# Attention cross term on 64x64 quarters of the array, states without zeros, features in another order

## The chip, the core and the metric

The kernel runs on one NeuronCore of a Trainium2 chip. A core has TensorE (PE in the profile, matmuls; its weight loads are PEld), VectorE (DVE), ScalarE (ACT), GpSimd (POOL) and SyncE (SP, whose queue issues most DMAs); sixteen DMA engines move data between HBM and the on-chip memory SBUF. Matmuls write to PSUM, 128 partitions with eight banks of 512 fp32 numbers each. The metric is device time in microseconds (us) of one execution, lower is better.

## What is computed

```python
def _attn_ref(q, k, v):                       # 8 batches, 8 heads, 576 tokens, head size 64, fp32
    scores = scale * np.matmul(q, k.transpose(0, 1, 3, 2))
    gamma = 1.0 - 2.0 ** (-5.0 - np.arange(H, dtype=np.float32))
    rel = pos[:, None] - pos[None, :]
    Dmat = np.where(rel >= 0, gamma[:, None, None] ** rel[None, :, :], 0.0)
    ret = scores * Dmat[None, :, :, :]
    return np.matmul(ret, v).astype(np.float32)

def reference(**kwargs):
    attn_out = _attn_ref(**attn_kwargs)
    x = np.ascontiguousarray(attn_out.transpose(0, 2, 1, 3)).reshape(B * S, H * D)
    x = _moe_ref(x=x, **moe_kwargs)           # 4608 tokens of 512 features, 8 experts, one for each token
    return _moe2_ref(x=x, **moe2_kwargs)      # soft mixture, 8 experts with 4 slots each
```

The attention has no softmax: each score is only multiplied by a power of gamma, which depends on the head and the distance. So it can be done in chunks of tokens: what lies inside a chunk by a masked score matrix, and everything before the chunk by one 64x64 state for each head (a sum of outer products of keys and values), which the queries of the chunk multiply. That product is called the cross term here.

## The kernel before

The attention is the first stage. Two batches form a pair, and a pair has nine chunks of 128 tokens: four of the first batch (c = 0 to 3), four of the second (c = 4 to 7), and a ninth (c = 8) that holds the last 64 tokens of both. Four pairs make 36 chunks, counted by g. Heads go in four pairs p, with h = 0 or 1 for the head in the pair; a pair of heads fills the 128 partitions (2 x 64 features).

A loop over g writes out the work by hand, and each engine runs its instructions in that order. For PE an iteration is: scores of chunk g+1 (`emit_S`, L179, each head on one half of the array's rows), cross term of g (`emit_cross`, L198 for c = 8 and L200), logits of g-2 (L223, into `ps_m`), token-major transposes of g-1 (L216), masked scores times values of g (`emit_AV`, L205, added to the cross term in the PSUM tile `ps_x`), state update of g (`emit_state`, L191), router gate of g-1 (`emit_gate`, L212). There is no cross term for c = 0 and 4, where a batch begins, and no state update for c = 8.

DVE masks the scores (L182, `st_s`), multiplies `ps_x` by powers of gamma (L209, `xT`) and works off the routing of groups of 3 to 5 chunks in small steps (L230 to L257; `r_rs`, L252, reads the ranks that PE has put into `ps_m`). ACT copies `xT`'s transposes (`xr`), the states (L193) and the gate's output (`ls`). POOL scales the values (`vh`) and scatters the routing table. In chunks 25 to 32 ACT and DVE also split the first expert's weights in two parts (`wh`, L287, and `wl`, L288). Six `kqv` buffers of 1 MB hold keys, queries and values; SP issues the load of chunk g+5 at the head of iteration g and then the other transfers of that iteration, in program order.

In the state tiles a pair of heads has a 128x128 square with the two heads' 64x64 states on the diagonal and zeros elsewhere, so one matmul with 128 rows and 128 columns does the cross term of two heads. The zeros are written once by POOL, and two ACT copies write the diagonal blocks. `ps_x` is one PSUM bank, with two buffers. Behind the attention come products of expert weights (`ps_w`, `ps_wt`, L277 and L282, the latter using `ps_x`'s buffers late), then the loop over expert slots, then the soft mixture.

Of the kernel before, what the change touches and what calls it, by code (L numbers as in the profile page):

```python
# [4 lines left out]
F32=mybir.dt.float32; F32R=mybir.dt.float32r; BF16=mybir.dt.bfloat16; I32=mybir.dt.int32; U32=mybir.dt.uint32  # L5
AF=mybir.ActivationFunctionType; ALU=mybir.AluOpType; AX=mybir.AxisListType
ET=mybir.EngineType
PSUM=bass.MemoryType.PSUM; DRAM=bass.MemoryType.DRAM
B,H,S,D=8,8,576,64
NP=4  # L10
NCH=9
NT=B//2*NCH
E,DM,FF=8,512,1024
# [3 lines left out]
NPF=6  # L17
# [6 lines left out]
def host(inp):  # L24
    f=np.float32; c=np.ascontiguousarray
    o={}
# [9 lines left out]
    ids=chunks(np.broadcast_to(np.arange(NTOK).reshape(B,1,S),(B,H,S)))[:,0]  # L36
    mid=np.asarray(inp['moe_modality_id'])
    o['mid']=c(mid[ids].T)
    wg=np.zeros((128,4,32),f); wg[:,:,:E]=inp['moe_w_gate'].reshape(4,128,E).transpose(1,0,2)
    o['wg']=wg  # L40
    o['mb']=c(inp['moe_modality_bias'].reshape(1,2*E))
    o['w2']=c(inp['moe_w2'].reshape(E,8,128,512).transpose(0,2,1,3))
# [2 lines left out]

    o['m1']=c(inp['moe2_w1'].reshape(2,4,4,128,1024).transpose(0,2,3,1,4)).reshape(8,128,2,2048)

    o['w1']=c(np.concatenate([inp['moe_w1'].reshape(E,4,128,2,512).transpose(0,2,3,1,4).reshape(E,128,2,2048),o['m1'][NPF:NPF+1]]))
    o['m2']=c(inp['moe2_w2'].reshape(2,4,2,4,128,2,256).transpose(5,0,2,4,3,1,6).reshape(8,128,4096))

    g=1.0-2.0**(-5.0-np.arange(H))
    pw=g[:,None]**np.concatenate([np.arange(S),np.arange(512,S)])[None]
    o['gt']=c(np.concatenate([np.repeat(x,64,axis=1).transpose(1,0,2).reshape(128,-1) for x in (pw[:,:128].reshape(NP,2,128),pw[:,0:640:128].reshape(NP,2,5))],axis=1).astype(f))
    o['vtab']=c((1.0/(8.0*pw)).reshape(H,5,128).transpose(2,1,0).astype(f))
    p=np.arange(128)
    cm=np.zeros((128,1028),f)
# [23 lines left out]
def body(nc,tc,I,O):  # L80
    V=nc.vector; G_=nc.gpsimd; A=nc.scalar; PE=nc.tensor; SP=nc.sync
# [7 lines left out]
    with ctx, tc.manual_schedule():  # L89
        pool=lambda st,name,bufs,**k: st.enter_context(tc.tile_pool(name=name,bufs=bufs,**k))  # L90
# [7 lines left out]
        raw=[WP.tile([128,2048],F32,name=f"raw{j}") for j in range(2)]; w2=WP.tile([128,8,512],F32,name="w2")  # L98
        Wall=WP.tile([128,E,256],F32,name="Wall")
        AT=ExitStack(); A1=pool(AT,"A1",1); A2=pool(AT,"A2",2);  # L100
        PS=ExitStack(); PS2=pool(PS,"PS2",2,space=PSUM); PS1=pool(PS,"PS1",1,space=PSUM)
        def splita(h):
            for c in range(4):
                s=slice(c*512,c*512+512)
# [8 lines left out]
        pw=PS1.tile([128,512],F32,name="ps_wu",tag="ps_t")  # L113
# [16 lines left out]
        gt=A1.tile([128,5,NP,128],F32,name="gt"); gr=A1.tile([128,NP,5],F32,name="gr")  # L130
# [10 lines left out]
        def decay(c):  # L141
            for h in range(2 if c==4 else 1):
                s=slice(64*h,64*h+64) if c==4 else slice(0,128); w=s.stop-s.start
                G_.tensor_tensor(out=gt[:,c,:,s],in0=gt[:,0,:,0:w],in1=bc(gr[:,:,c],[128,NP,w],2),op=ALU.mult)
        state=[A1.tile([128,NP,128],F32,name=f"st{j}") for j in range(4)]
        for t in state: G_.memset(t,0.0)
        gk=A1.tile([128,NT,TW],F32,name="gk"); G_.memset(gk,0.0); idx=A1.tile([128,NT],U32,name="idx")
        cum=A1.tile([128,len(GR),E],BF16,name="cum"); spare=A1.tile([1,1],F32,name="spare")
        bias=A1.tile([128,NT,E],F32,name="bias")
# [11 lines left out]
        vh={}  # L161
        def pk(g,j): return kqv[g][:,j].rearrange("q (p t) -> q p t",p=NP)
        def pos_(g): return (0,1,2,3,0,1,2,3,4)[g%NCH]
        rq=[]
        def tick(n=1,stop=True):
            for _ in range(n):
                if rq and not (stop and rq[0].__name__=="rank"): rq.pop(0)()
# [5 lines left out]
        sts={}; xps={}; xTs={}; lss={}; pst={}  # L173
        def qT(g,p): return pk(g,1)[:,p]
# [9 lines left out]
        def emit_state(g):  # L184
            c=g%NCH; v=vh[g]; kt=kqv[g][:,3]
            if c%4==0: pst[0]=PS1.tile([128,NP,D],F32,name="ps_st")
            ps=pst[0]
            for p in range(NP):
                for h in range(2):
                    hh=2*p+h  # L190
                    PE.matmul(out=ps[64*h:64*h+64,p],lhsT=kt[:,hh*D:hh*D+D],rhs=v[:,hh],start=c%4==0 and p==0,stop=p==NP-1,skip_group_check=True)  # L191
            for h in range(2):
                r=slice(64*h,64*h+64); A.copy(out=state[2+c//4 if c%4==3 else c%2][r,:,r],in_=ps[r])  # L193
        def emit_cross(g):
            c=g%NCH; xps[g]=PS2.tile([128,NP,128],F32,name="ps_x")
            if c==8:
                for h in range(2):
                    for p in range(NP): PE.matmul(out=xps[g][:,p,64*h:64*h+64],lhsT=state[2+h][:,p],rhs=qT(g,p)[:,64*h:64*h+64],start=h==0 and p==0,stop=False,skip_group_check=True)  # L198
            elif c%4:
                for p in range(NP): PE.matmul(out=xps[g][:,p],lhsT=state[(c-1)%2][:,p],rhs=qT(g,p),start=p==0,stop=False)  # L200
        def emit_AV(g):
            c=g%NCH; ps=xps[g]; v=vh[g]
            for p in range(NP):
                for h in range(2):
                    PE.matmul(out=ps[64*h:64*h+64,p],lhsT=v[:,2*p+h],rhs=sts[g,h][:,p],start=c in(0,4) and p==0,stop=p==3,skip_group_check=c==8)  # L205
            for h in range(2): sts.pop((g,h))
        def emit_x(g):
            t=A2.tile([128,NP,128],F32,name="xT")
            V.tensor_tensor(out=t,in0=xps.pop(g),in1=gt[:,pos_(g)],op=ALU.mult); xTs[g]=t; tick()  # L209
        def emit_gate(g):  # L210
            lp=PS1.tile([128,128],F32,name="ps_gt")
            for j in range(4): PE.matmul(out=lp[32*j:32*j+32],lhsT=wg[:,j],rhs=xTs[g][:,j],start=True,stop=True)  # L212
# [65 lines left out]
            if c==3:  # L278
                t=A1.tile([128,256],F32,name="wt",bufs=2); A.copy(out=t,in_=wps.pop(e)); wts[e]=t
        def emit_WT(e,late=False):  # L280
            pt=PS2.tile([128,256],F32,name="ps_wt",tag="ps_x") if late else PS1.tile([128,256],F32,name="ps_wt",tag="ps_t"); t=wts.pop(e)
            for h in range(2): PE.transpose(out=pt[:,h*128:h*128+128],in_=t[:,h*128:h*128+128],identity=ident)  # L282
            A.copy(out=Wall[:,e],in_=pt)
        def split(h,cs=range(4)):
# [417 lines left out]
```

## Time and profile before

| | us |
|---|---|
| median of three runs | 666.62 (663.51 to 666.94) |
| the profiled execution, its own time | 665.61 |
| its span in the profile | 664.0 |
| PE busy | 613.2 |
| DVE, ACT, POOL busy | 319.0, 220.1, 247.7 |

The span is what the profiler saw, from the program's first instruction to its last. Times of rows are counted from its start. The attention is over at about 178 us; the first expert's transposes begin at 198.05 us. An fp32 matmul of the program is two PE instructions in the trace, each with its own weight load.

### The profile page before, as it was taken

The page shows a single profiled execution, that of the slowest core. Times are in us where ns is not written, and L with a number is a line of the kernel's source. Part 1 is how long each engine was busy: PE and PEld are TensorE (multiplying, and loading weights), DVE is VectorE, ACT ScalarE, POOL GpSimd, SP SyncE. Part 2 cuts the span into 40 slices and gives each one's busy share as a digit, 9 for nine tenths or more (in the row PEclk, how much of TensorE's full clock was granted, in tenths as well). Part 3 has the DMA queues.
Part 4 walks back from the last instruction along what each step waited for, and adds up shares of the span by engine and source line. Part 5 has one row for each costly group of instructions (what it writes and reads, how often), then busy time and mean ns, then how long its engine had stood idle before and what let it go on. Part 6 is the DMA issues. An engine that isn't in the chain of part 4 may idle for free. (4 is left out here: it accounts for less than half of the span.)

```text
span 664.0 us, 17074 instructions
## 1 busy us (share of the span) xinstructions
PE 613.2 (92%) x5866; PEld 461.1 (69%) x5866; DVE 319.0 (48%) x934; ACT 220.1 (33%) x577; POOL 247.7 (37%) x355
## 2 busy tenths in 40 slices
PE   7999999999969999988999999999998999669984
PEld 5888888888637766755677777777775777453453
DVE  2355555567434434566544544555555544322343
ACT  1333333344315233354233233332353233211332
POOL 4524445355536432466244334433455344110000
PEclk7999999999988999988999999999999999888995
DMA  8999999985928860144654444444404401857888
GB/s 291 414 378 386 418 387 323 352 317 208 394 90 332 287 245 16 37 146 161 258 162 144 142 149 153 162 163 151 163 21 161 162 11 51 294 211 282 356 284 286
DMA packets 48244, 148.53 MB, mean 224 GB/s; under 512 B 12276, under 2 KB 23935, under 8 KB 37888
## 3 DMA queue, kind: packets, MB, share of 16 engines
q1 hardware_dynamic: 41936, 132.60, 55.3%
q0 software_dynamic: 6192, 14.53, 6.3%
q8 instruction: 55, 0.90, 0.6%
q14 instruction: 61, 0.50, 0.2%
HBM read 291.93 MB, written 27.71 MB: 481 GB/s over the span
## 5 line engine op out<-in xcount | busy, mean ns | idle before, releaser
L472 PE MATMUL ps_L<-wh,xl 128*128 128x512 f32 x624 | 212.3, 412 | 0.9 <-ACTq L529 0.9
L472 PEld LDWEIGHTS ps_L<-wh,xl 128*128 128x128 f32 x624 | 116.0, 191 | 38.6 <-issue 16.9
L472 PE MATMUL ps_L<-wl,xl 128*128 128x512 f32 x312 | 126.5, 405 | 4.9 <-PEq L529 1.5
L472 PEld LDWEIGHTS ps_L<-wl,xl 128*128 128x128 f32 x312 | 59.4, 190 | 32.1 <-issue 22.0
L476 DVE TENSOR_SCALAR hh<-ps_L,gi 128x512 f32<-128x512 f32 x39 | 29.3, 750 | 97.4 <-PE ps_L L472 97.3
L182 DVE TENSOR_TENSOR st_s<-ps_s,cm 128x512 f32<-128x512 f32 x72 | 47.7, 683 | 38.2 <-PE ps_s L179 31.9
L170 POOL TENSOR_TENSOR vh<-kqv,vtab 128x512 f32<-128x512 f32 x36 | 37.3, 1036 | 71.1 <-PE ps_st L191 51.2
L494 ACT ACTIVATE z<-ps_z,mt 32x128 f32<-32x128 f32 x39 | 14.0, 358 | 148.2 <-DVE mt L493 148.2
L508 POOL TENSOR_SCALAR cy<-cx,cm 128x32 f32<-128x32 f32 x39 | 14.4, 369 | 123.9 <-DVE cm L507 119.6
L509 POOL DMA_INDIRECT cs<-cy,ui x39 | 42.2, 1083 | 16.5 <-POOL cy L508 13.3
L179 PE MATMUL ps_s<-kqv 64*128 64x128 f32 x576 | 44.1, 292 | 2.0 <-DVE st_s L182 1.6
L260 POOL DMA_INDIRECT tb<-gk,idx x36 | 36.0, 1001 | 19.2 <-issue 4.9
L179 PEld LDWEIGHTS ps_s<-kqv 64*128 64x128 f32 x576 | 36.8, 193 | 8.5 <-issue 3.6
L481 PE MATMUL ps_h<-cs__103,hh 128*128 128x128 f32 x312 | 41.3, 276 | 0.0
L209 DVE TENSOR_TENSOR xT<-ps_x,gt 128x512 f32<-128x512 f32 x36 | 24.8, 690 | 32.4 <-PE ps_x L205 29.2
L205 PE MATMUL ps_x<-st_s,vh 128*64 128x128 f32 x576 | 40.3, 283 | 0.0
L217 ACT COPY xr<-ps_t 128x512 f32<-128x512 f32 x36 | 21.0, 585 | 57.9 <-PE ps_t L216 57.9
L475 ACT ACTIVATE hh<-ps_L,gi 128x512 f32<-128x512 f32 x39 | 26.9, 689 | 32.1 <-PE ps_L L472 32.1
L453 POOL DMA_INDIRECT xr__2862<-xd,ui x28 | 29.4, 1051 | 20.2 <-POOL ui L452 8.7
L481 PEld LDWEIGHTS ps_h<-cs__103,hh 128*128 128x128 f32 x312 | 36.2, 143 | 0.1
L205 PEld LDWEIGHTS ps_x<-st_s,vh 128*64 128x64 f32 x576 | 31.4, 139 | 6.1 <-issue 6.1
L193 ACT COPY st<-ps_st 64x256 f32<-64x256 f32 x64 | 23.4, 366 | 29.5 <-PE ps_st L191 28.9
(238 smaller groups left out, 1017.7 us busy)
## 6 DMA issues: line engine op xcount, KB each, us to landing
raw<-in_w SPq DMA_DIRECT2D x79, 1024.0 KB
w<-in_w SPq DMA_DIRECT2D x38, 2048.0 KB
kqv<-in_qkv SPq DMA_DIRECT2D x28, 1024.0 KB
m<-in_m SPq DMA_DIRECT2D x19, 1024.0 KB
xd<-xr SPq DMA_DIRECT2D x32, 256.0 KB
wh<-mx SPq DMA_DIRECT2D x8, 1024.0 KB
wl<-mx SPq DMA_DIRECT2D x8, 1024.0 KB
w2T<-in_w2T SPq DMA_DIRECT2D x12, 512.0 KB
```

The costliest lines, as they stand in the source:

```text
L170: G_.tensor_tensor(out=t,in0=kqv[g][:,2].rearrange("p (h d) -> p h d",h=H),in1=bc(vtab[:,pos_(g)],[128,H,D],2),op=ALU.mult)
L179: r=slice(64*h,64*h+64); PE.matmul(out=pss[h][:,p],lhsT=pk(g,0)[r,p],rhs=pk(g,1)[r,p],start=True,stop=True)
L182: V.tensor_tensor(out=st,in0=pss[h],in1=bc(masks[g%NCH],[128,NP,128],1),op=ALU.mult)
L205: PE.matmul(out=ps[64*h:64*h+64,p],lhsT=v[:,2*p+h],rhs=sts[g,h][:,p],start=c in(0,4) and p==0,stop=p==3,skip_group_check=c==8)
L209: V.tensor_tensor(out=t,in0=xps.pop(g),in1=gt[:,pos_(g)],op=ALU.mult); xTs[g]=t; tick()
L260: nodep(G_.indirect_dma_start(out=tb,out_offset=bass.IndirectOffsetOnAxis(ap=idx[:,k:k+1],axis=0),in_=gk[:,k],in_offset=None),"tb")
L453: G_.indirect_dma_start(out=xg[i%3],out_offset=None,in_=xd,in_offset=bass.IndirectOffsetOnAxis(ap=u,axis=0),bounds_check=NTOK-1,oob_is_err ...
L472: PE.matmul(out=ps,lhsT=a[:,c],rhs=w[h][:,s],start=n==0,stop=n==11); n+=1; m+=1
L475: if h==0: A.activation(out=d,in_=q,func=AF.Relu,scale=g)
L476: else: V.tensor_scalar(out=d,in0=q,scalar1=0.0,scalar2=g,op0=ALU.max,op1=ALU.mult)
L481: for c in range(4): PE.transpose(out=ps[:,c],in_=hh[i%2][:,2*half+c//2,(c%2)*128:(c%2)*128+128],identity=ident)
L509: nodep(G_.indirect_dma_start(out=cs,out_offset=bass.IndirectOffsetOnAxis(ap=gi[i][1],axis=0),in_=y,in_offset=None,bounds_check=NTOK-1,oob ...
```

## The change

The cross term is done by a 64x64 matmul for each head, with the state on half of the array's rows (by h) and the result on half of its columns (by p%2): four heads lie on the four quarters. A state tile is [128,4,64] and needs no zeros, and one ACT copy writes it. `ps_x` is [128,2,512], two banks of which 256 columns each are used: the head h of a pair picks the bank, since the two row halves write at the same time. It comes from the pool with one buffer, where it had two. The features of a token get another order, (p%2 and head size) on partitions, (h, p//2) along the tile; the router's weights, the first expert layer and the gamma table are permuted to match on the host. The loops of `emit_AV` are nested the other way round.

```diff
+    perm=np.arange(DM).reshape(2,2,2,D).transpose(2,0,1,3).reshape(-1)
+    wg=np.zeros((128,4,32),f); wg[:,:,:E]=inp['moe_w_gate'][perm].reshape(4,128,E).transpose(1,0,2)
...
-        PS=ExitStack(); PS2=pool(PS,"PS2",2,space=PSUM); PS1=pool(PS,"PS1",1,space=PSUM)
+        PS=ExitStack(); PS1=pool(PS,"PS1",1,space=PSUM)
...
-        state=[A1.tile([128,NP,128],F32,name=f"st{j}") for j in range(4)]
-        for t in state: G_.memset(t,0.0)
+        state=[A1.tile([128,NP,D],F32,name=f"st{j}") for j in range(4)]
...
+            A.copy(out=state[2+c//4 if c%4==3 else c%2],in_=ps)
+        def xo(g,p,h): return xps[g][64*(p%2):64*(p%2)+64,h,128*(p//2):128*(p//2)+128]
+        def emit_cross(g):
+            c=g%NCH; xps[g]=PS1.tile([128,2,512],F32,name="ps_x")
+            for a in range(2) if c==8 else (0,) if c%4 else ():
+                t=slice(64*a,64*a+64) if c==8 else slice(0,128)
+                for p in range(NP):
+                    for h in range(2):
+                        r=slice(64*h,64*h+64)
+                        PE.matmul(out=xo(g,p,h)[:,t],lhsT=state[2+a if c==8 else (c-1)%2][r,p],rhs=qT(g,p)[r,t],start=a==0 and p<2,stop=False,skip_group_check=True)
+        def emit_AV(g):
+            c=g%NCH; v=vh[g]
             for h in range(2):
-                r=slice(64*h,64*h+64); A.copy(out=state[2+c//4 if c%4==3 else c%2][r,:,r],in_=ps[r])
-        def emit_cross(g):
-            c=g%NCH; xps[g]=PS2.tile([128,NP,128],F32,name="ps_x")
-            if c==8:
-                for h in range(2):
-                    for p in range(NP): PE.matmul(out=xps[g][:,p,64*h:64*h+64],lhsT=state[2+h][:,p],rhs=qT(g,p)[:,64*h:64*h+64],start=h==0 and p==0,stop=False,skip_group_check=True)
-            elif c%4:
-                for p in range(NP): PE.matmul(out=xps[g][:,p],lhsT=state[(c-1)%2][:,p],rhs=qT(g,p),start=p==0,stop=False)
-        def emit_AV(g):
-            c=g%NCH; ps=xps[g]; v=vh[g]
-            for p in range(NP):
-                for h in range(2):
-                    PE.matmul(out=ps[64*h:64*h+64,p],lhsT=v[:,2*p+h],rhs=sts[g,h][:,p],start=c in(0,4) and p==0,stop=p==3,skip_group_check=c==8)
+                for p in range(NP):
+                    PE.matmul(out=xo(g,p,h),lhsT=v[:,2*p+h],rhs=sts[g,h][:,p],start=c in(0,4) and p<2,stop=p>1,skip_group_check=True)
             for h in range(2): sts.pop((g,h))
         def emit_x(g):
             t=A2.tile([128,NP,128],F32,name="xT")
-            V.tensor_tensor(out=t,in0=xps.pop(g),in1=gt[:,pos_(g)],op=ALU.mult); xTs[g]=t; tick()
+            V.tensor_tensor(out=t.rearrange("q (h n) t -> q h (n t)",h=2),in0=xps.pop(g)[:,:,0:256],in1=gt[:,pos_(g)].rearrange("q (h n) t -> q h (n t)",h=2),op=ALU.mult); xTs[g]=t; tick()
...
-            pt=PS2.tile([128,256],F32,name="ps_wt",tag="ps_x") if late else PS1.tile([128,256],F32,name="ps_wt",tag="ps_t"); t=wts.pop(e)
+            pt=PS1.tile([128,256],F32,name="ps_wt",tag="ps_x") if late else PS1.tile([128,256],F32,name="ps_wt",tag="ps_t"); t=wts.pop(e)
```

No engine gets its blocks in another order. What stands inside the cross term's block changes, and what it waits for. On PE, in the iteration of a chunk near the start, before, with the semaphores that an instruction waits for (Activation is ACT's, Pool is POOL's):

```order
L200 MATMUL ps_x<-kqv,st_132 128x128 [waits Activation_49]
L200 MATMUL ps_x<-kqv,st_132 128x128 x3
L223 MATMUL ps_m<-cs__103,ls 128x8 [waits Activation_49]
L216 MATMUL ps_t<-cs__103,xT 128x128 [waits DVE_49]
L216 MATMUL ps_t<-cs__103,xT 128x128 x3
```

And the same place now (the line numbers are one higher from here on):

```order
L201 MATMUL ps_x<-kqv,st_129 64x128 [waits DVE_49,Activation_49]
L201 MATMUL ps_x<-kqv,st_129 64x128 x7
L224 MATMUL ps_m<-cs__100,ls 128x8 [waits Activation_49]
L217 MATMUL ps_t<-cs__100,xT 128x128 x4
L206 MATMUL ps_x<-st_s,vh 64x128 [waits Pool_49]
```

Four matmuls have become eight, and DVE's `xT` of the chunk before, which the transposes waited for, is now waited for by the first matmul of the cross term. On ACT, in two iterations, before:

```order
L193 COPY st_131<-ps_st 64x4x64 x2
L213 COPY ls<-ps_gt 128x128
L217 COPY xr<-ps_t 128x512
L193 COPY st_132<-ps_st 64x4x64 x2
L213 COPY ls<-ps_gt 128x128
```

And now:

```order
L192 COPY st_128<-ps_st 128x256
L214 COPY ls<-ps_gt 128x128
L218 COPY xr<-ps_t 128x512
L192 COPY st_129<-ps_st 128x256
L214 COPY ls<-ps_gt 128x128
```

The two state copies of each chunk are one, and what stands behind them keeps its place.

## Rows read from the trace of the kernel before

**Rows 1.** The page: busy time by engine (PE's line), granted clock in 40 slices.
```profile
PE 613.2 (92%) x5866; PEld 461.1 (69%) x5866; DVE 319.0 (48%) x934; ACT 220.1 (33%) x577; POOL 247.7 (37%) x355
...
PEclk7999999999988999988999999999999999888995
```

**Rows 2.** Busy time in stretches, us from the span's start; the columns are named.
```profile
core 0: us, PE busy (x) PEld busy (x) DVE busy (x) ACT busy (x) POOL busy (x), PEclk, DMA share, GB/s
0.00:50.00 50.00, 46.02 (x593) 38.61 (x595) 19.94 (x38) 13.33 (x32) 20.38 (x33) 0.93 0.96 361
50.00:60.00 10.00, 10.00 (x162) 8.47 (x162) 5.40 (x13) 3.23 (x8) 3.38 (x5) 1.00 1.03 382
...
13.00:178.00 165.00, 163.06 (x2443) 141.16 (x2439) 90.33 (x224) 60.62 (x152) 76.51 (x114) 1.00 0.95 358
190.00:200.00 10.00, 3.87 (x41) 2.06 (x40) 2.02 (x8) 2.11 (x6) 4.26 (x7) 0.78 0.26 64
```

**Rows 3.** Waits of PE, 10 to 200 us: total us, times, longest.
```profile
PE ps_m L223 <- DVE r_rs L252: 1.3, 3, 0.5
PE ps_x L200 <- ACT st L193: 0.7, 1, 0.7
```

**Rows 4.** Timeline, one chunk: start, us, engine, line, what; then idle time before.
```profile
122.80 0.63 PE L191 MATMUL ps_st<-vh,kqv 128*64 128x64 f32 x16
123.02 0.69 DVE L209 TENSOR_TENSOR xT<-ps_x,gt 128x512 f32<-128x512 f32 x1 [1.46 <-PE ps_x L205]
123.36 0.16 PEld L212 LDWEIGHTS ps_gt<-xT,wg 128*32 128x32 f32 x8
123.72 0.97 PEld L179 LDWEIGHTS ps_s<-kqv 64*128 64x128 f32 x16 [0.20 <-issue]
124.81 0.97 PEld L200 LDWEIGHTS ps_x<-kqv,st 128*128 128x128 f32 x8
125.70 0.30 PEld L223 LDWEIGHTS ps_m<-cs__103,ls 128*128 128x128 f32 x2
```

**Rows 5.** Timeline, the cross term of the first ninth chunk (c = 8).
```profile
47.31 1.86 PEld L198 LDWEIGHTS ps_x<-kqv,st 128*128 128x128 f32 x16
...
49.09 0.30 PEld L223 LDWEIGHTS ps_m<-cs__103,ls 128*128 128x128 f32 x2
```

**Rows 6.** Timeline, the iteration behind the first ranked routing group.
```profile
56.36 1.16 PE L200 MATMUL ps_x<-kqv,st 128*128 128x128 f32 x8
...
57.07 0.19 DVE L252 TENSOR_TENSOR r_rs<-ps_m,r_ob 128x40 f32<-128x40 f32 x1
...
57.40 0.36 PE L223 MATMUL ps_m<-cs__103,ls 128*128 128x8 f32 x2
```

**Rows 7.** Timeline, the same behind the fifth group, where weights are split too.
```profile
137.87 0.62 ACT L287 CAST wh<-raw 128x512 fp32r<-128x512 f32 x1
...
138.53 0.69 DVE L288 TENSOR_TENSOR wl<-raw,wh 128x512 fp32r<-128x512 f32 x1 [1.37 <-ACT wh L287]
...
140.07 0.36 PE L223 MATMUL ps_m<-cs__103,ls 128*128 128x8 f32 x2 [0.41 <-DVE r_rs L252]
```

**Rows 8.** Timeline, the first cross term.
```profile
15.11 0.76 ACT L193 COPY st<-ps_st 64x256 f32<-64x256 f32 x2
...
15.92 1.16 PE L200 MATMUL ps_x<-kqv,st 128*128 128x128 f32 x8 [0.66 <-ACT st L193]
```

**Rows 9.** Timeline, from the last weight transposes to the first expert's.
```profile
192.36 0.37 ACT L283 COPY Wall<-ps_wt 128x256 f32<-128x256 f32 x1
192.50 0.20 PEld L282 LDWEIGHTS ps_wt<-cs__103,wt 128*128 128x128 f32 x2 [0.42 <-ACT wt L279]
...
193.13 0.27 DVE L397 MEMSET Gs<- 128x257 f32 x1 [6.60 <-PE ps_wt L282]
...
198.05 0.48 PE L459 MATMUL ps_xT<-cs__103,xr__2862 128*128 128x128 f32 x1 [5.11 <-DMA xr__2862<-xd,ui]
```

**Rows 10.** Timeline of SP's queue, 41 to 53 us, and PE at 64.67 us.
```profile
41.37 0.33 SPq L123 DMA_DIRECT2D kqv<-in_qkv  x1
41.79 9.34 SPq L159 DMA_DIRECT2D tb<-w2T  x9
...
52.39 1.05 SPq L123 DMA_DIRECT2D kqv<-in_qkv  x1
...
64.67 1.16 PE L179 MATMUL ps_s<-kqv 64*128 64x128 f32 x16
```

More of the change, by code (lines that the diff above doesn't have):

```diff
@@ L38, in host @@
     o['mid']=c(mid[ids].T)
-    wg=np.zeros((128,4,32),f); wg[:,:,:E]=inp['moe_w_gate'].reshape(4,128,E).transpose(1,0,2)
+    perm=np.arange(DM).reshape(2,2,2,D).transpose(2,0,1,3).reshape(-1)
+    wg=np.zeros((128,4,32),f); wg[:,:,:E]=inp['moe_w_gate'][perm].reshape(4,128,E).transpose(1,0,2)
     o['wg']=wg
@@ L46, in host @@
     o['m1']=c(inp['moe2_w1'].reshape(2,4,4,128,1024).transpose(0,2,3,1,4)).reshape(8,128,2,2048)
-    o['w1']=c(np.concatenate([inp['moe_w1'].reshape(E,4,128,2,512).transpose(0,2,3,1,4).reshape(E,128,2,2048),o['m1'][NPF:NPF+1]]))
+    o['w1']=c(np.concatenate([inp['moe_w1'][:,perm].reshape(E,4,128,2,512).transpose(0,2,3,1,4).reshape(E,128,2,2048),o['m1'][NPF:NPF+1]]))
     o['m2']=c(inp['moe2_w2'].reshape(2,4,2,4,128,2,256).transpose(5,0,2,4,3,1,6).reshape(8,128,4096))
@@ L52, in host @@
     pw=g[:,None]**np.concatenate([np.arange(S),np.arange(512,S)])[None]
-    o['gt']=c(np.concatenate([np.repeat(x,64,axis=1).transpose(1,0,2).reshape(128,-1) for x in (pw[:,:128].reshape(NP,2,128),pw[:,0:640:128].reshape(NP,2,5))],axis=1).astype(f))
+    o['gt']=c(np.concatenate([np.repeat(x,64,axis=1).transpose(1,0,2).reshape(128,-1) for x in [y.reshape(2,2,2,-1).transpose(2,0,1,3).reshape(4,2,-1) for y in (pw[:,:128],pw[:,0:640:128])]],axis=1).astype(f))
     o['vtab']=c((1.0/(8.0*pw)).reshape(H,5,128).transpose(2,1,0).astype(f))
```

## Prediction

> **What bounds the kernel now.** I read the page first: TensorE (PE) is busy for 92% of the span, no other engine for half of it, and the granted clock is full for almost all of it [rows 1]. The change lies in the attention stage alone, so I read the time in stretches next: from 13 to 178 us PE is busy for 163.06 of 165 us at granted clock 1.00, the 2.4 GHz level, but the sixteen DMA engines have a share of 0.95 there too, and 1.03 in the stretch at 50 us [rows 2]. Both could be the limit. The list of waits decides for PE: from 10 to 200 us it waited 1.3 us for DVE's `r_rs` and 0.7 us for ACT's state copy, and no wait for a `kqv` load stands there [rows 3]. So in this stage the sum of PE's work is the time, and a nanosecond saved there counts unless another engine is next in line.
>
> The timeline of one chunk gives the prices [rows 4]. Counted from the first weight load of a block to that of the next: cross term 124.81 to 125.70 = 0.89 us, scores (L179) 123.72 to 124.81 = 1.09, the state block 122.80 to 123.36 = 0.56, the gate 123.36 to 123.72 = 0.36. An fp32 matmul stands in the trace as two instructions, so the cross term's 4 are 8 rows: 0.89/8 = 0.111 us for one pass of 128 columns through the array; I call it a step. The scores have 16 instructions on 64 rows each, in pairs on the two row halves: 8 steps = 0.89, and 0.20 more. The gate has 8 on 32 array columns each, four side by side: 2 steps = 0.22, and 0.14 more. So row halves do run in pairs, column quarters do run four at a time, and what is left, 0.14 to 0.20, is the price of going from one division of the array to another (drain, and the first weights loaded in the open). The cross term pays none now, since the logit matmul behind it uses the whole array too.
>
> **The change, part by part.**
>
> *Plain cross terms.* Chunks 1, 2, 3, 5, 6, 7 of four batch pairs, 24 in all. Now 8 matmuls on 64x64 quarters, 16 instructions. If four run at a time they are 4 steps = 0.44, plus one more change of division behind them, 0.17 as the middle of 0.14 and 0.20: 0.61. Saved 0.89 - 0.61 = **0.28** each (0.25 to 0.31). No row shows row and column halves at once; the pairs and fours above are the nearest.
>
> *Six of the 24 give little.* Where a routing group was ranked in the iteration before, the next logit matmul writes `ps_m`, from which DVE's `r_rs` still has to read. At 56 us: cross at 56.36, `r_rs` 57.07 to 57.26, logit at 57.40, just when the cross term would have let it go (56.36 + 1.00) [rows 6]. A shorter cross term there becomes a wait. I found six such places (55, 73, 96, 114, 137, 156 us). Four give about 0.03 each. In the last two DVE comes later still, PE already waits 0.41, and the way to `r_rs` leads over ACT's `wh` copy and DVE's `wl` [rows 7]; ACT now makes two state copies of 64x256 in 0.76 us and then one of 128x256. A copy of 128x256 out of PSUM takes 0.37 elsewhere [rows 9], as long as one half does, so `wh` comes 0.37 earlier and these two give 0.37 each. Six together: **0.8**. The other 18 give 18 x 0.28 = **5.0**.
>
> *Chunk 8 of each pair*, the two tails of 64 tokens: 8 matmuls on the whole array, 16 instructions, 47.31 to 49.09 = 1.78 us [rows 5]. That is 0.111 a step although only 64 columns pass: the 128-column weight load sets it. Then 16 matmuls on quarters, 8 steps with 64 weight columns and 64 moving ones. The state block has just these sizes in pairs: 0.56 for 8 steps with a change, 0.053 to 0.07 a step. At 0.06: 0.48 + 0.17 = 0.65, saved 1.13, times four = **4.5** (bounds: 1.2 each at 0.053; 0.7 each if a step stays at 0.111).
>
> *State.* The copy loses its second half. At the first cross term PE waits 0.66 for the second copy [rows 8]; one copy ends 0.38 earlier: **0.4**. Elsewhere the state has been there before the scores end, and the other 31 second copies of 0.37 cost nothing. The zeroing of four state tiles by POOL at the start is covered by the wait for the first load.
>
> *One buffer in place of two.* `ps_x` takes two banks (a row half writes its own bank), so there is one of it, and the cross term must wait until DVE's `xT` of the chunk before has read it. `xT` ends at 123.02 + 0.69 = 123.71, the cross term begins at 124.81 [rows 4]: 1.10 us of cover, made of state, gate and scores, none of which shrinks. Cost 0. Without that cover it would be one `xT`, 0.69, per chunk. Queued behind it on PE would be logit, token transposes and AV, for which ACT and then the stores wait. At the very end the last two weight transposes (L282) share this tile: the second starts at 192.50 now and would wait for ACT's `Wall` copy, 192.36 + 0.37 = 192.73, and everything up to the first gather (PE waits until 198.05) hangs behind it [rows 9]: **-0.3**.
>
> AV's eight matmuls come in another order, still alternating column halves: 0. DVE reads as many elements of `ps_x`: 0. The permuted weights are made on the host.
>
> *Loads.* The saving makes PE use `kqv` earlier while the DMA engines are full. The tightest place is chunk 13: its load is issued at 52.39, behind nine pieces of `tb` that held the queue from 41.79, and its scores begin at 64.67 [rows 10]. By 50 us 361 GB/s x 50 = 18.1 MB had moved, then 382 GB/s [rows 2]; I count 20.9 MB issued up to and with that load, which makes it land near 57.5, about 7 us ahead. PE will have gained some 3.5 us by then. Cost 0; 2 us if my count is 5 us off.
>
> Sum: 5.0 + 0.8 + 4.5 + 0.4 - 0.3 = 10.4. The profiled execution took 665.61 (span 664.0), so 655.2; it is 1.0 under the median of the three runs, 666.62, and I take **655.6**.
>
> **Rivals.**
>
> *A. Instructions set the pace, not columns.* The state block's 32 matmuls and weight loads in 0.56 could be an issue limit: 0.035 us per matmul row. Then a plain cross term takes 16 x 0.035 + 0.17 = 0.73 (saves 0.16), a tail one 32 x 0.035 + 0.17 = 1.29 (saves 0.49): 2.9 + 0.8 + 2.0 + 0.1 = 5.8, about 660. Against it: the gate passes 8 in 0.22, 0.027 each, and 128-column steps explain that alone. The Trainium skill, page "TensorE: Matmul & The Clock Gate", section on 56 ns against 53.3 ns, says that with hardware decoding off the sequencer spends about 62 ns on each matmul; by that figure, an estimate, 16 would need 0.99 us and 32 would need 1.98, and the kernel would take about 673. This trace does not agree, the state block has a matmul every 35 ns, so I give that case 0.01.
>
> *B. Only pairs run together.* Cross 8 x 0.111 + 0.17 = 1.06, 0.17 worse; tails 16 x 0.06 + 0.17 = 1.13, 0.65 better. -3.1 - 0.6 + 2.6 + 0.1 = -1.0: 666.6, no change. For it: no row of two row halves and two column halves at once, with four moving streams to four quarters. Against: the scores write two banks at once, the gate reads four streams at once.
>
> *C. The quarters run one by one (slower).* Cross 16 x 0.111 + 0.17 = 1.95, 1.06 worse, times 24; tails 32 x 0.06 + 0.17 = 2.09, 0.3 worse: 26 us, 692. With a step of s for 128 columns and 0.54 s for 64, the gain is 18 x (0.72 - 4 s) + 4 x (1.61 - 4.3 s) + 0.9 = 20.3 - 89 s: above s = 0.23, twice what I assume, the change loses.
>
> *D. The freed time meets loads.* If the rate of 358 to 382 GB/s [rows 2] cannot follow chunks that are 0.28 shorter, PE waits for `kqv` near chunks 13 to 17, and 2 to 4 us of the 10 are lost: 658 to 660.
>
> **How the numbers follow.** My forecast 0.70, with its own range 652 to 658 (bounds above, and the three runs lie 3.4 us apart); a gain above it 0.03; A and D together 0.12; B 0.09; C 0.05; the 62 ns case 0.01. Leaving out the low end, most of B and C gives a range of 651 to 661. What a measurement of this kernel can tell from no change is about 0.5%, 3.3 us: faster means below 663.3. Forecast, larger gain, A and D are faster: 0.85; B is the same: 0.09; C with the 62 ns case is slower: 0.06.
>
> **What the profile after would show.** Cross blocks of 0.6 us from first weight load to the next block's, 0.65 in chunk 8; logit matmuls waiting for `r_rs` at all six places, some 0.25 us more at the first four; a chunk of 4.36 us in place of 4.64; no idle time of PE before the cross block on `xT`, and none before scores on `kqv`; the first gather's transpose near 188 in place of 198. Cross blocks of 1.1 or more would be B or C. The prediction is wrong if the later stage does not move to the left by what attention saves, for instance because the clock falls elsewhere at the turn: that stretch has 0.78 granted already [rows 2].

## The result, and the profile after

The changed kernel took 652.74 us, median of four runs (650.26 to 654.82), against 665.07 us (661.62 to 666.94) for the kernel before in the four runs beside it: a ratio of 0.984 [0.980, 0.987], 12.3 us less. A later set of runs of the same changed kernel gave 648.84 against 662.02, 0.980 [0.975, 0.985]. The profiled execution took 651.03 us, span 649.4, against 665.61 and 664.0 before.

From the page: TensorE has 14.9 us less to do and still the same share of the span, 92% [rows 1].

```profile
PE 598.3 (92%) x6122; PEld 441.1 (68%) x6122; DVE 319.1 (49%) x934; ACT 208.5 (32%) x545; POOL 245.9 (38%) x351
...
PEclk8999999999979999988999999999999999889997
```

One chunk after, from the timeline, in the order of [rows 4], with the masked scores times values (L206) of this chunk and the next at its ends:

```profile
113.19 0.85 PEld L206 LDWEIGHTS ps_x<-st_s,vh 128*64 128x64 f32 x16 [0.17 <-issue]
...
114.34 0.69 DVE L210 TENSOR_TENSOR xT<-ps_x,gt 128x512 f32<-128x512 f32 x1 [0.73 <-PE ps_x L206]
...
115.04 0.97 PEld L179 LDWEIGHTS ps_s<-kqv 64*128 64x128 f32 x16 [0.20 <-issue]
...
116.13 0.43 PEld L201 LDWEIGHTS ps_x<-kqv,st 64*64 64x64 f32 x16
...
116.73 0.30 PEld L224 LDWEIGHTS ps_m<-cs__100,ls 128*128 128x128 f32 x2 [0.17 <-issue]
...
117.53 0.53 PEld L206 LDWEIGHTS ps_x<-st_s,vh 128*64 128x64 f32 x10 [0.17 <-issue]
```

The cross block lasts 116.13 to 116.73 = 0.60 us, where it was 0.89; the scores are still 1.09. The chunk lasts 117.53 - 113.19 = 4.34. DVE's `xT` ends at 115.03 and the next cross term starts at 116.13, so the cover of the single `ps_x` is 1.10 us, as before. The cross term of the first ninth chunk, from the timeline of PE's weight loads, is 0.63 where [rows 5] have 1.78:

```profile
47.37 0.56 PEld L201 LDWEIGHTS ps_x<-kqv,st 64*64 64x64 f32 x32
48.00 0.30 PEld L224 LDWEIGHTS ps_m<-cs__100,ls 128*128 128x128 f32 x2
```

PE's waits from 10 to 200 us, the first four lines and the one on the weight transposes, to hold against [rows 3]:

```profile
PE ps_m L224 <- DVE r_rs L253: 3.1, 7, 0.6
PE ps_x L206 <- POOL cum L155: 2.2, 1, 2.2
PE ps_xT L460 <- DMA xr__2950<-xd,ui: 1.8, 1, 1.8
PE ps_L L473 <- ACTq L530: 0.9, 1, 0.9
...
PE ps_wt L283 <- ACT Wall L284: 0.5, 1, 0.5
```

The wait for the state copy is gone, that for `r_rs` has grown from 1.3 to 3.1, no `kqv` load and no `xT` has come in. The line of 2.2 us on POOL is new, and the wait for the first gather (`xr`) is 1.8 us where it was 5.11 [rows 9].

To see where the 14.6 us between the two profiled spans went, I cut both at PE instructions that both have: the masked scores times values of chunks 1, 5 and 35, and the first expert's transposes. Starts are read from the timeline; the table holds their differences, in us, for all kernels that ran, the experiments included.

| kernel | start to chunk 1 | 1 to 5 | 5 to 35 | 35 to expert | expert to end |
|---|---|---|---|---|---|
| before | 17.44 | 17.66 | 138.85 | 24.10 | 465.91 |
| after | 15.22 | 20.54 | 129.44 | 21.09 | 463.06 |
| after, once more | 17.12 | 16.77 | 129.44 | 21.51 | 460.80 |
| order by pairs (e3) | 17.10 | 18.02 | 129.82 | 20.46 | 465.34 |
| order by quarters (e10) | 15.80 | 20.26 | 129.96 | 21.34 | 465.40 |
| two halves (e7) | 17.26 | 18.48 | 143.35 | 19.39 | 462.96 |
| padded states (e2) | 18.21 | 16.77 | 129.43 | 24.54 | 464.45 |
| before, with a pad (e9) | 17.37 | 17.66 | 138.83 | 20.14 | 463.95 |
| preparation moved (e1) | 17.17 | 16.77 | 129.44 | 20.95 | 465.01 |
| ranking earlier (e4) | 16.50 | 20.26 | 128.74 | 20.99 | 464.88 |
| both of these (e6) | 16.41 | 16.77 | 127.78 | 20.30 | 466.38 |
| two state copies (e8) | 16.89 | 17.91 | 130.25 | 20.29 | 466.50 |

The changed kernel gained 9.41 us in chunks 5 to 35, as the cross-term part of the prediction has it. But it also gained 3.01 in the stretch to the first expert, where the prediction has a loss of 0.3, and lost 2.88 in chunks 1 to 5, where it has a gain. The first and last columns vary by 3 and 6 us between kernels that hardly differ there, the two runs of the changed kernel among them, so single values in them are not read as effects.

The loss first. The timeline of POOL and PE around chunk 4, and the stretches at the start and around chunk 4:

```profile
27.30 0.22 POOL L154 CAST mf<-mid 128x36 f32<-128x36 int32 x1 [7.18 <-DMA mid<-in_mid]
...
28.78 1.05 POOL L170 TENSOR_TENSOR vh<-kqv,vtab 128x512 f32<-128x512 f32 x1
...
29.88 1.93 PE L206 MATMUL ps_x<-st_s,vh 128*64 128x128 f32 x16 [2.17 <-POOL cum L155]
```

```profile
core 0: us, PE busy (x) PEld busy (x) DVE busy (x) ACT busy (x) POOL busy (x), PEclk, DMA share, GB/s
5.00:17.00 12.00, 10.49 (x141) 8.84 (x140) 5.13 (x8) 1.14 (x3) 4.90 (x5) 0.86 1.01 362
29.00:36.00 7.00, 6.12 (x82) 5.16 (x84) 1.98 (x3) 0.77 (x3) 5.18 (x8) 0.76 1.00 378
30.00:33.00 3.00, 3.00 (x40) 2.68 (x40) 0.69 (x1) 0.24 (x1) 2.63 (x5) 0.50 1.04 401
```

POOL stood still for 7.18 us until the load of `mid` landed; only behind that preparation did it scale chunk 4's values (`vh`, to 29.83), and PE waited 2.17 us for them. Right behind this wait the granted clock is low: 0.50, the 1.2 GHz level, from 30 to 33 us and 0.76 over 29 to 36 us, and the block of 16 that takes 1.09 at full clock takes 1.93. The kernel before has the same load, preparation and values in this order, but its chunk 4 began only at 30.46. In this run PE started early: 5 to 17 us had a granted clock of 0.86.

Then the gain at the turn to the experts, from the timeline, to hold against [rows 9]; the first line is the first gather before, which [rows 9] do not have, the others are after:

```profile
194.84 1.07 POOL L453 DMA_INDIRECT xr__2862<-xd,ui  x1 [5.05 <-DVE xr__2862 L427]
```

```profile
177.78 0.27 DVE L398 MEMSET Gs<- 128x257 f32 x1
...
183.04 1.07 POOL L454 DMA_INDIRECT xr__2950<-xd,ui  x1 [1.00 <-DMA gi<-tb]
...
184.03 0.44 PE L283 MATMUL ps_wt<-cs__100,wt 128*128 128x128 f32 x2 [0.46 <-ACT Wall L284]
...
186.29 0.66 PE L460 MATMUL ps_xT<-cs__100,xr__2950 128*128 128x128 f32 x4 [1.82 <-DMA xr__2950<-xd,ui]
```

The last weight transposes do wait for ACT's copy, 0.46 us, as foretold. But DVE's clearing of `Gs`, which in the kernel before stood 6.60 us for these transposes and had the rest of DVE's clearing behind it, now comes 6 us ahead of them and waits for nothing. Before, POOL's first gather waited 5.05 us for that clearing (of `xr`); now it waits for the load of its indices (`gi`). So nothing on the way to the first gather hangs on the transposes any more.

### The profile page after: what moved, and what is told of

Its sections match the earlier page's. It is cut to its first block, busy times and chain, and to the rows that moved or that the text cites. A ratio compares the mean times of both kernels' runs of the same rounds, so it can differ in the third digit from the quotient of the medians.

```text
span 649.4 us, 17574 instructions
## 1 busy us (share of the span) xinstructions
PE 598.3 (92%) x6122; PEld 441.1 (68%) x6122; DVE 319.1 (49%) x934; ACT 208.5 (32%) x545; POOL 245.9 (38%) x351
## 5 line engine op out<-in xcount | busy, mean ns | idle before, releaser
L206 PE MATMUL ps_x<-st_s,vh 128*64 128x128 f32 x576 | 41.1, 287 | 2.2 <-POOL cum L155 2.2
L206 PEld LDWEIGHTS ps_x<-st_s,vh 128*64 128x64 f32 x576 | 32.1, 141 | 8.3 <-issue 5.7
L462 DVE TENSOR_TENSOR xl<-ps_xT,xl 128x512 fp32r<-128x512 f32 x40 | 27.2, 681 | 10.6 <-ACT xl L462 10.6
```

Of the source, the lines that this page charges most:

```text
L206: PE.matmul(out=xo(g,p,h),lhsT=v[:,2*p+h],rhs=sts[g,h][:,p],start=c in(0,4) and p<2,stop=p>1,skip_group_check=True)
L462: A.copy(out=hi,in_=ps); V.tensor_tensor(out=lo,in0=ps,in1=hi.bitcast(F32),op=ALU.subtract)
```

## The experiments

My theory: four quarters at a time are worth what the sum says (9 to 10 us), the smaller state tiles have moved what lies behind them in SBUF and so removed a wait of DVE (3 us), and a late load under an early chunk 4 gives part of it back. The rivals: the gain is not the quarters but instruction pace or the copies; the tail's 3 us come from the shorter attention itself; the clock alone makes the loss at chunk 4.

### Do the quarters run at once, and does the order matter? (e3, e10, e7)

The order by pairs puts the four matmuls of one half of the columns ahead of the four of the other half:

```diff
-                for p in range(NP):
+                for p in (0,2,1,3):
                     for h in range(2):
```

> The changed kernel with the same sixteen instructions for a cross term in the order p = 0, 2, 1, 3, so that neighbours in the queue need the same half of the array's columns and only the two row halves can run together. Theory (the gain is that four quarters run at once): a cross block takes 8 x 0.111 + 0.17 = 1.06 us in place of 0.60, chunk 8's about 1.13 in place of 0.63; 18 plain ones and four tails add 8.3 + 2.0, of which 1.4 vanish in the wait at chunk 4: about 662. Rival (the gain comes from smaller weight loads and the single state copy, whatever the order): no more than 655.

It took 650.64 us (649.40 to 652.38), 0.979 [0.975, 0.983] of the kernel before. The block did not grow; from the timeline of PE:

```profile
120.05 0.68 PE L201 MATMUL ps_x<-kqv,st 64*64 64x128 f32 x16
120.66 0.39 PE L224 MATMUL ps_m<-cs__100,ls 128*128 128x8 f32 x2
```

0.61 us against 0.60: the expectation missed. I took the order further and put all of one quarter's work in front of the next quarter's:

```diff
-                for p in range(NP):
-                    for h in range(2):
+                for h in range(2):
+                    for p in (0,2,1,3):
```

> The changed kernel with the cross term's matmuls in the order of the quarters: both matmuls of one quarter, then both of the next (h outside, p = 0, 2, 1, 3 inside), so that up to four passes in a row need the same quarter. Theory (each quarter works off its own list, and a matmul for a free quarter passes those that wait for a busy one; the run in the order 0, 2, 1, 3 took 0.61 us a block): a block still takes about 0.65 us, 0.60 plus a few times the 0.026 us that the start of the third and fourth quarter came later in that run; the kernel 652 to 654. Rival (matmuls start in the program's order, and the earlier run was saved by something else): 16 x 0.111 less a little overlap, 1.4 to 1.9 us a block, the kernel 670 or more.

It took 653.30 us (648.99 to 654.42), 0.983 [0.978, 0.989]. From the timeline of PE:

```profile
116.71 0.69 PE L201 MATMUL ps_x<-kqv,st 64*64 64x128 f32 x16
117.32 0.39 PE L224 MATMUL ps_m<-cs__100,ls 128*128 128x8 f32 x2
```

0.61 again. The same timeline up to 116.86 us shows that only four of the sixteen have started by then (at 116.71 to 116.75); the next four start at 116.87:

```profile
116.71 0.36 PE L201 MATMUL ps_x<-kqv,st 64*64 64x128 f32 x4
```

The first four in the program all belong to one quarter, and two quarters start no more than two at a time, as the halves below show; so these four lie on different quarters. If a matmul could not start before the one ahead of it in the program has started, each quarter would begin when the quarter before it is at its last step, and the block would last about 13 steps of 0.111, 1.4 us. So, by this working, matmuls of a free quarter pass those that wait for a busy one, and each quarter has its own line. The Trainium skill, page "TensorEngine Tiling (Array Packing)", section "Key Properties", says that tiles operate independently; these two blocks agree. Its page "TensorE: Matmul & The Clock Gate", section "The mechanism", says that matmuls keep the program's order in start and end; for these quarters the block of 0.61 does not agree.

What if only two quarters have work at a time? Here the cross term is split in two: the matmuls of one column half stay in their place, those of the other half come behind the token transposes, with the same number of matmuls in all:

```diff
-        def emit_cross(g):
+        def emit_cross(g,half):
...
-                for p in range(NP):
+                for p in (half,half+2):
...
-            emit_cross(g)
+            emit_cross(g,0)
...
-            emit_AV(g); emit_x(g)
+            emit_cross(g,1); emit_AV(g); emit_x(g)
```

> The changed kernel with each cross term cut in two: the head pairs p = 0, 2 (one half of the array's columns, so two quarters) where it stands, p = 1, 3 behind the token transposes, so that never more than two quarters can run at once. Theory (the gain is four quarters at once): a part takes as long as the whole, 4 steps and a change of division, 0.61 us, so each of the 24 plain terms costs 0.61 more and each of the four tails 0.65 more; AV to AV of chunks 5 to 35 takes 129.4 + 20 x 0.61 + 4 x 0.65 = 144, the kernel about 667. Rival (16 instructions cost what they cost, about 0.44 in all, whichever quarters they use): half of the block and one more change, 0.17 to 0.33 more each: 134 to 138, the kernel 657 to 661.

It took 663.95 us (661.90 to 665.17, ten runs): 0.999 [0.997, 1.001], no gain left. From its timeline of PE:

```profile
120.70 0.65 PE L202 MATMUL ps_x<-kqv,st 64*64 64x128 f32 x8
121.28 1.09 PE L207 MATMUL ps_x<-st_s,vh 128*64 128x128 f32 x16
...
124.22 0.65 PE L202 MATMUL ps_x<-kqv,st 64*64 64x128 f32 x8
124.80 0.39 PE L225 MATMUL ps_m<-cs__100,ls 128*128 128x8 f32 x2
```

Half of the instructions on two quarters take 0.58 us, as long as all of them on four. The timeline up to 120.85 us shows that they start two at a time (the next two come at 120.86):

```profile
120.70 0.33 PE L202 MATMUL ps_x<-kqv,st 64*64 64x128 f32 x2
```

An instruction pace would give half of the time to half of the instructions. Chunks 5 to 35 take 143.35, where 144 was expected from quarters that run four at a time and at most 138 from a pace. The whole was expected at 667; this execution had no wait at chunk 4, on which that number still counted.

### Where the 3 us at the turn come from (e2, e9)

The changed kernel with state tiles as large as before, half of them unused:

```diff
-        state=[A1.tile([128,NP,D],F32,name=f"st{j}") for j in range(4)]
+        state=[A1.tile([128,2,NP,D],F32,name=f"st{j}")[:,0] for j in range(4)]
```

> The changed kernel with state tiles that take as many bytes as before (half of them unused), so that what is laid out behind them in SBUF lies where it lay before. Theory (3 us of the gain come from the layout: DVE's first clearing of the next stage no longer overlaps the tiles of the last weight transposes and so doesn't wait for them): the clearing of Gs waits for the last transposes again, the first expert's transposes wait about 5 us for the gather in place of 1.8, and the kernel takes about 655.5. Rival (the gather came sooner because less was on the DMA engines): no change, 652 to 653.

It took 655.55 us (653.83 to 656.61), 0.987 [0.983, 0.991]. From its timeline, DVE and PE at the turn:

```profile
183.88 0.27 DVE L398 MEMSET Gs<- 128x257 f32 x1 [6.88 <-PE ps_wt L283]
...
188.95 1.11 PE L460 MATMUL ps_xT<-cs__100,xr__2950 128*128 128x128 f32 x4 [5.26 <-DMA xr__2950<-xd,ui]
```

The wait is back, and the stretch from chunk 35 to the expert is 24.54, near the 24.10 of the kernel before, with the attention of the changed kernel, so the shorter attention is not its cause. The counterpart is the kernel before with unused bytes behind its states:

```diff
         for t in state: G_.memset(t,0.0)
+        pad=A1.tile([128,2048],F32,name="pad")
```

> The kernel before the change, with one unused tile of 8 KB a partition behind the states and nothing else. It moves what is laid out behind it, so that the clearing of Gs, the gather's buffers and the others no longer overlaps the tiles of the last weight transposes. Theory (3 us of the change's gain are layout alone, free to the old kernel too): the first expert's transposes wait about 1.8 us for the gather in place of 5.1, and the kernel takes about 661 where the kernel before takes 664. Rival: the gather is held by something else, and nothing moves.

It took 658.55 us (656.67 to 659.95), 0.991 [0.988, 0.994], with the old cross term and unused bytes alone: 5.8 us less than the kernel before beside it, where 3 was expected. From its timeline:

```profile
186.44 0.27 DVE L398 MEMSET Gs<- 128x257 f32 x1
...
194.00 0.66 PE L460 MATMUL ps_xT<-cs__103,xr__2863 128*128 128x128 f32 x4 [1.15 <-DMA xr__2863<-xd,ui]
```

`Gs` is cleared without a wait, and the stretch is 20.14, 3.96 less. In its profiled execution the stretch behind it is 1.96 shorter too, within the scatter of that column, so only the 3.96 are put down to the pad. That `Gs` had come to lie on memory that the transposes still read is the likely reason; addresses were not looked at.

### The wait at chunk 4 (e1, and the changed kernel once more)

The preparation that needs `mid` is skipped in iteration 2 and done twice in iteration 3, behind the values of chunk 4:

```diff
-            if prepare and g: prepare.pop(0)()
+            for _ in range({2:0,3:2}.get(g,1)):
+                if prepare and g: prepare.pop(0)()
```

> The changed kernel, but POOL does the two preparations that need the late load of the modality ids (L154, L155) one iteration later, behind the scaled values of chunk 4 instead of ahead of them. Theory (the gain of the first cross terms was lost at chunk 4, where PE waited 2.2 us for the scaled values, which stood on POOL behind that load, and the clock then fell for 3.4 us): AV of chunk 4 starts near 27.6 us instead of 29.9, the wait of 2.2 us is gone, chunk 5's AV starts 3 to 3.5 us earlier, and the kernel takes about 649.5 against 652.7. Rival (chunk 4 was late because its own load was late): the wait stays, under another name, and the time stays at 652 to 653.

It took 651.32 us (648.53 to 652.09), 0.980 [0.975, 0.984]. From its timeline:

```profile
23.21 1.04 POOL L170 TENSOR_TENSOR vh<-kqv,vtab 128x512 f32<-128x512 f32 x1 [1.34 <-issue]
26.87 0.22 POOL L154 CAST mf<-mid 128x36 f32<-128x36 int32 x1 [2.61 <-DMA mid<-in_mid]
...
29.59 1.09 PE L206 MATMUL ps_x<-st_s,vh 128*64 128x128 f32 x16
```

Chunk 4's values are scaled 3.7 us ahead of the preparation that waits for the late load, PE's block starts without a wait and takes 1.09; at 29.59 it is 2.0 us behind the time expected, since this execution reached chunk 1 that much later. Chunks 1 to 5 take 16.77 in place of 20.54. The total of the profiled execution did not follow (650.98 us), for two reasons that the table shows: chunk 1 came 1.95 us later, and the stretch behind the gather was 1.95 us longer. To see how much of the wait is luck of the start, I ran the changed kernel unaltered again:

> The changed kernel itself once more, unchanged, on the same chip and beside the same runs of the kernel before. Expected if the first result holds: 652 to 654, 11 to 12.5 us under the kernel before; from AV to AV of chunks 5 to 35 129.4 us again, and from chunk 1 to 5 between 16.8 and 20.5, more the earlier chunk 1 comes, since POOL's late load sets when chunk 4 can go on. If the first result was chance, the difference lies under 9 or over 15.

648.84 us (647.28 to 650.95), 0.980 [0.975, 0.985]. From its timeline:

```profile
28.36 1.04 POOL L170 TENSOR_TENSOR vh<-kqv,vtab 128x512 f32<-128x512 f32 x1
...
29.55 1.09 PE L206 MATMUL ps_x<-st_s,vh 128*64 128x128 f32 x16
```

The values come almost as late, but PE reaches chunk 4 later, since it reached chunk 1 at 17.12 and not at 15.22, and does not wait: 16.77 again, at a granted clock of 1.00 over 29 to 36 us. It is at chunk 5 at 33.89 us, 1.87 earlier than the profiled execution that had started 1.90 earlier (15.22 + 20.54 = 35.76).

The wait has two ends, and both move. Where PE does not wait, it takes 12.43 us from chunk 1 to chunk 4 (17.12 to 29.55); and in the old order chunk 4's values are ready 2.53 us behind the start of the preparation (27.30 to 29.83). In the order by pairs PE was at chunk 1 at 17.10, as here, but POOL could go on only at 28.18 in place of 26.87, and PE waited:

```profile
28.18 0.22 POOL L154 CAST mf<-mid 128x36 f32<-128x36 int32 x1 [7.53 <-DMA mid<-in_mid]
...
30.77 1.09 PE L206 MATMUL ps_x<-st_s,vh 128*64 128x128 f32 x16 [1.15 <-POOL cum L155]
```

By the same sums the moved preparation above proves little: with chunk 1 at 17.17 and the preparation at 26.87 the old order would have had the values at 29.40, ahead of PE at 29.60. The version further down that moves the preparation and a ranking step (e6) tells more:

```profile
27.10 0.22 POOL L154 CAST mf<-mid 128x36 f32<-128x36 int32 x1 [3.60 <-DMA mid<-in_mid]
...
28.84 1.09 PE L206 MATMUL ps_x<-st_s,vh 128*64 128x128 f32 x16
```

PE was at chunk 1 at 16.41 and at chunk 4 at 28.84 without a wait; the old order would have had the values at 29.63. So the order of preparation and values makes the wait; that moving it makes the kernel faster is not shown by the times.

The clock is not the cause by itself, but it adds to the loss. In the order by pairs and with two copies (e8) PE waited 1.15 and 1.08 us, the clock over 29 to 36 us stayed at 1.00, and chunks 1 to 5 took 1.25 and 1.14 more than 16.77: little more than the wait. In the profiled execution, the order by quarters and the earlier ranking (e4) it waited 2.17, 1.83 and 1.94, the clock there was 0.76, and the three lost 3.77, 3.49 and 3.49.

### The waits for the rankings, and the copies (e4, e6, e8)

More of DVE's routing steps in each iteration, so that `r_rs` comes earlier:

```diff
-            if ready: tick(1,False)
+            if ready: tick(1,False); tick(2)
```

> The changed kernel, but DVE does the two steps that read the ranks (r_rs, r_po) right behind PE's ranking, at the end of the iteration, where DVE is idle, and not behind the next mask. Theory (in the six iterations behind a ranking the shorter cross term only became a wait of the logit matmul for r_rs): these waits, 0.35 to 0.6 each, are gone, the cross terms there give their 0.29 as well, and the kernel takes about 650.5 against 652.7. Rival (DVE is the limit in those iterations, so the wait moves on to the masks or to AV): 652 to 653.

It took 652.07 us (648.96 to 655.13), 0.981 [0.976, 0.987]. PE's waits for `r_rs` fell from 3.1 to 0.4 us, but chunks 5 to 35 became only 0.70 shorter: the rival of the expectation came about, and the waits moved on. The timeline says why:

```profile
59.85 1.48 DVE L233 TENSOR_TENSOR r_d<-r_l,r_mx 128x32 f32<-128x32 f32 x1
60.23 1.04 POOL L170 TENSOR_TENSOR vh<-kqv,vtab 128x512 f32<-128x512 f32 x1
...
61.86 1.76 DVE L236 SCALAR_TENSOR_TENSOR r_oh<-r_d,cm 128x32 f32<-128x32 f32 x1
...
62.51 1.05 POOL L170 TENSOR_TENSOR vh<-kqv,vtab 128x512 f32<-128x512 f32 x1
...
64.79 1.05 POOL L170 TENSOR_TENSOR vh<-kqv,vtab 128x512 f32<-128x512 f32 x1
64.80 1.09 DVE L250 TENSOR_SCALAR r_sm<-r_sm 128x4 f32<-128x4 f32 x1
...
66.62 0.67 PE L201 MATMUL ps_x<-kqv,st 64*64 64x128 f32 x16 [0.74 <-DVE gk L251]
```

Three small steps of DVE, on 32 or 4 numbers a partition, took 1.48, 1.76 and 1.09 us where the others of that stretch take 0.16 to 0.20, and each ends 0.05 or 0.06 us after a scaling of values on POOL that overlaps it (61.27 and 61.33; 62.51 + 1.05 = 63.56 and 63.62; 65.84 and 65.89). What DVE does next is late by as much, and PE's cross term waits for DVE. It depends on the step: in chunks 5 to 35 of this run ten steps over 0.3 us long met the scaling, all of them `r_d` and `r_oh`, which read two SBUF tiles, or the TENSOR_SCALAR of `r_sm`, and all ended 0.03 to 0.06 us behind it; 31 reductions, reciprocals and steps that read PSUM met it too and took 0.17 to 0.20. The Trainium skill, page "SBUF — State Buffer", section "SBUF: two separate sides", says that DVE, in a two-port mode or with two SBUF inputs, and GpSimd arbitrate for a shared port pair, and that the loser stands until the other's instruction is through; the ends of these rows agree. The first two steps had begun 0.38 and 0.65 us ahead of the scaling, during a scatter on POOL; why they did not end before it is not shown.

One more step in place of two, together with the moved preparation:

```diff
-            if prepare and g: prepare.pop(0)()
+            for _ in range({2:0,3:2}.get(g,1)):
+                if prepare and g: prepare.pop(0)()
...
-            if ready: tick(1,False)
+            if ready: tick(1,False); tick()
```

> The changed kernel with POOL's preparation one iteration later (as in the run on the preparation), and DVE's first rank step alone (r_rs, one step instead of two) right behind PE's ranking. Theory (the six waits for r_rs are pure order; the run that moved two steps lost 1.7 us where DVE's small steps then fell on POOL's scatter): the waits go from 3.1 us to about 0.4, chunks 5 to 35 take 127.3 us from AV to AV in place of 129.4, and the kernel takes about 648. Rival (DVE's steps collide with POOL's scatter or scaling wherever they are moved to): 129 us, about 650.5.

649.07 us (648.74 to 649.28), 0.978 [0.975, 0.980] of the kernel before. Chunks 5 to 35 take 127.78, 1.66 less than in the changed kernel. From the list of PE's waits, 10 to 200 us:

```profile
PE ps_x L201 <- ACT st L192: 1.1, 2, 0.6
...
PE ps_m L224 <- DVE r_rs L253: 0.4, 1, 0.4
```

2.7 us of waits for `r_rs` are gone, 1.1 for the state copy have come: 1.6, which is the gain. It is the best version by its trace in the attention; its interval and that of the changed kernel run again (0.975 to 0.985) overlap, so the times alone don't place it ahead.

The last one gives ACT its two state copies back:

```diff
-            A.copy(out=state[2+c//4 if c%4==3 else c%2],in_=ps)
+            for h in range(2):
+                r=slice(64*h,64*h+64); A.copy(out=state[2+c//4 if c%4==3 else c%2][r],in_=ps[r])
```

> The changed kernel with the state copied out of PSUM in two halves of 64 partitions, as before. Theory (one copy saves 0.37 where ACT stands on the way to r_rs, behind the rankings near 131 and 149 us, and nothing elsewhere): AV to AV of chunks 5 to 35 takes 0.74 more, 130.2 us, the kernel 653.5, which the times alone will hardly tell. Rival (ACT's shorter work counts in more places, and is part of what the quarters got the credit for): 2 us or more.

653.83 us (646.45 to 655.30), 0.982 [0.975, 0.989]; chunks 5 to 35 take 130.25, 0.81 more than with one copy, where 0.74 more was expected. The single copy is worth that, and 8.6 of the 9.4 us are not its doing.

## Why the prediction was right, by its own steps

The measured 652.74 lies 2.9 us below the predicted 655.6 and inside the range. That it is so near is in part luck: the cross terms came out as summed, but two things of 3 us or more were left out of the sum, in opposite directions. The later set of runs, 648.84, lies below the range; it is 13.2 us under the kernel before beside it, where the prediction has 11.0.

*Plain cross terms.* Predicted 0.61 a block and 0.28 saved, measured 0.60 and 0.29. *Ninth chunks.* Predicted 0.65 and 1.13, measured 0.63 and 1.15. Between chunks 5 and 35 lie 14 of the plain cross terms, all six behind a ranking and all four ninth chunks: predicted 14 x 0.28 + 0.8 + 4 x 1.13 = 9.2, measured 9.41. Taken chunk by chunk, from the starts of the masked scores times values before and after, the 14 give 4.16, the four 4.54, and *the six behind a ranking*, in their order, 0.01, 0.01, 0.00, 0.01, 0.36 and 0.34, where four times 0.03 and twice 0.37 were predicted; the waits for `r_rs` grew as told, by 1.8 us in all. In the run with two copies the last two give 0.00 each, so what they gave comes from the single state copy, as predicted. The three plain cross terms between chunks 1 and 5 show in every run of the four quarters in the first order that had no wait at chunk 4: 17.66 - 16.77 = 0.89, 0.30 each.

*State and the single buffer.* The wait for the first copy is gone from the list; its 0.4 us can't be told from the scatter of the start. No cross term waits for `xT`, the cover is 1.10 as counted. *Loads.* No wait for `kqv` stands in the list, so rival D did not come about.

*The last weight transposes*, -0.3, is the step that failed. The wait came, 0.46 long, but "everything up to the first gather hangs behind it" no longer held. The stretch gained 3.01, and the cause is not the cross term: smaller tiles moved other tiles, and a clearing that used to wait for the transposes did not any more. Restoring the size brought the wait back; a pad in the kernel before removed it there. I had the row with that wait of 6.60 us before me [rows 9] and did not ask whether the change of a tile's size could end it. My sum of 10.4, which knows nothing of the layout, gives 655.2; the version with the padded states took 655.04 in its profiled execution. This, too, is near by luck in part: its median is 8.5 us under the kernel before beside it (664.01).

*What was missing* is chunk 4: I looked for a transfer behind `kqv` that PE would reach too early, and not for one that POOL waits for in front of work that PE needs. In the profiled execution it cost 20.54 - 16.77 = 3.77 us, in the second one none.

*The rivals.* B and C would have shown blocks of 1.06 and 1.95, the measured one is 0.60. A asked for 0.73 and 1.29; 0.60 and 0.63 refute it, and so does the version with halves. In the ninth chunk 32 matmul rows pass in 0.63, 0.020 us each, so the 0.035 of the state block was no limit of instructions. The sentence on the first gather held roughly: 186.29, near the 188 that was told, by the same two errors, which partly cancel, and a start that was 2.22 us earlier.

## What to carry to other kernels

Where a matmul has blocks of zeros in it, cutting it into quarters pays in the ratio of steps, less one change of the array's division for each block; price it from blocks of the same trace that already use halves. When an edit changes the size of a tile, look through the list of waits for those between buffers that have nothing to do with each other: they can go or come with the layout, and here one of them was worth a third of what the edit itself gave. When an engine gets faster, look at what the other engines do in front of the work that it needs, waits for loads above all. And before a run counts as proof that a wait is gone, work out from its own times whether the wait would have come at all.

## What the runs showed of the hardware that was not expected

- A block on the four 64x64 quarters took 0.60 to 0.61 us in each of the three orders in which the program named the quarters, and half of it, on two quarters, took 0.58.
- In three executions PE waited 1.83, 1.94 and 2.17 us at chunk 4, and the granted clock over 29 to 36 us was 0.76; in one of them a block of 1.09 took 1.93. In two others it waited 1.08 and 1.15, and the clock stayed at 1.00.
- Small DVE steps of 0.16 to 0.20 us took 0.55 to 1.76 us when they met POOL's scaling of values and read two SBUF tiles or were a TENSOR_SCALAR on four numbers; reductions and steps that read PSUM did not grow.
- The start up to chunk 1 took between 15.22 and 18.21 us and the part behind the first gather between 460.8 and 466.5 us in kernels that hardly differ there. The two executions that reached chunk 1 first, at 15.22 and 15.80, had a granted clock of 0.86 in 5 to 17 us, the ten others 0.72 to 0.74. Why an execution starts one way or the other, and what makes the later part vary, stays open.
